# Weight-block sums of the last expert moved from VectorE to GpSimd, in the second phase of an attention and mixture-of-experts kernel

## Chip, cores and metric

The kernel runs on one core of a Trainium2 chip. The metric is device time in microseconds (us) of one execution; lower is better. Engines are named as in the profile: PE is TensorE (PEld its weight loads), DVE VectorE, ACT ScalarE, POOL GpSimd, and SP the engine that issues most DMAs.

## What is computed

The reference is a linear attention with a complex decay, followed by a dense mixture of four experts:

```
for t in range(768):                       # 4 batches, 8 heads, head size 48
    S_re, S_im = ar*S_re - ai*S_im + k_t v_t^T, ar*S_im + ai*S_re
    y[t] = q_t @ S_re
x = y as [3072, 384]
p = domain_probs / (sum + 1e-9)
out = sum over e of p[:, e] * (relu(x @ w1[e]) @ w2[e])     # w1[e] 384 x 1024, w2[e] 1024 x 384
```

All data are float32. The matmuls run on values rounded to a shorter float32 format; each operand is split into a high part and a low part (the difference), and a product is made of three matmuls: high by high, low by high, high by low.

## The kernel before, in words

**Two phases.** In the first, the attention is computed in 12 groups of 256 time steps while experts 0 and 1 are applied to the groups that are done (lines 229 and 209 are their matmuls). The second phase applies experts 2 and 3 with a bilinear scheme of rank 20: a unit multiplies four blocks of 128 hidden columns by two blocks of 384 rows over three blocks of inner dimension, 24 block products, and does it with 20 products of sums of blocks. Each product needs a sum of 128 x 128 weight blocks (the weight operand, splits in `shi` and `slo`, two of them in `ext`) and a sum of 384-column blocks of `x` (`xh`, `xl`).

**Rounds and units.** Each of the two experts takes four rounds, R = 0 to 3 for expert 2 and R = 4 to 7 for expert 3; each round covers 768 rows of `x`. A round has two units, h = 0 and h = 1, one for each half of the hidden layer. The order of a unit is written out in the table UNIT: "M" is a product (three matmuls into one of five PSUM banks `pb`, 0 to 4), "C" a copy of a bank by ScalarE, "D" a sum or difference by VectorE into a bank or into the buffer `SN`, "H" and "L" the high and low part of a finished hidden block (`hid`), "F" eight places where second-layer matmuls of an earlier block (`pob`) are put, and "B" a place where up to n steps of background work are issued.

**Background work.** The list `side` holds what has to be prepared for later units; `bg(n)` takes up to n steps from its head. A step of kind "sum" or "split" counts one; a step of kind "pool" counts nothing and is issued as soon as it is at the head. A "gap" of k stops k calls that still have steps left to take. A split is two instructions: ScalarE writes the high part and VectorE the low part; the ScalarE half of the following split is issued ahead of the VectorE half of this one. What is left in the list at the end of an h = 0 unit is issued there, all at once.

**Order on the engines.** In the second phase ScalarE, VectorE and SP instructions are held in the order in which the program issues them, and so are TensorE's. GpSimd's are not: a scheduler orders them. Each engine runs its queue in order, so an instruction that waits holds up all that stand behind it on its engine.

**What is prepared.** `prep_x(R+1)` (sums of `x` blocks on GpSimd, from line 896, and splits) for each next round. `prep_w(e, h, ...)` for weights: it loads four weight rows (SP, line 973) into the first half of `ACC` and into `RX`, makes 15 sums in the scratch `s`, which lies in the columns 2304 and up of `Z`, splits the sums and some raw blocks, and loads the second-layer weights by casting DMAs on GpSimd (line 995), whose low parts are finished in the h = 1 unit (line 999 and a ScalarE instruction each). Both halves of expert 2 are prepared at the end of the first phase. The first half of expert 3 is prepared in R = 1, h = 0, long before it is used in R = 4, h = 0. The second half is prepared in R = 4, h = 0 and used in R = 4, h = 1, directly behind it.

**Lines.** Line 890 is `tt` (VectorE sums and the low parts of splits), 893 `stt` (VectorE low parts of hidden blocks and the accumulation), 887 `act` (ScalarE copies and high parts), 896 `pool` (GpSimd sums), 884 `pe` (matmuls of the second phase), 1091 and 1123 the loads and stores of the accumulator `ACC`, 1018 the loads of `x` blocks.

Of the kernel before, what the change touches and what calls it, by code (L numbers as in the profile page):

```python
# [28 lines left out]
E1 = 2  # L29
# [20 lines left out]
TB2 = 384  # L50
# [48 lines left out]
def fast_path(ctx, tc, qkP, aP, vP, probsP, w, out, flag):  # L99
# [11 lines left out]
                            base=32, channel_multiplier=1)  # L111
# [148 lines left out]
    with ExitStack() as c1:  # L260
# [4 lines left out]
        def tmp(name):  # L265
# [6 lines left out]
                                base=0, channel_multiplier=-1)  # L272
# [70 lines left out]
        last = {}  # L343
# [436 lines left out]
        x = {}  # L780
# [79 lines left out]
    with ExitStack() as c2:  # L860
# [4 lines left out]
        Z = fin.tile([P, 11 * TB2], F32, name="Z")  # L865
        SN = fin.tile([P, 7 * TB2], F32, name="SN")
        ACC = fin.tile([P, 2 * C2 * HD], F32, name="ACC")
        RX = fin.tile([P, TB2], F32, name="RX")
# [3 lines left out]
        side, freed, ready = [], set(), set()  # L872

        def cut(n):
            return slice(n * P, (n + 1) * P)
# [4 lines left out]
        def pin(ins):  # L880
            return tc.keep_in_program_order(ins) if held["on"] else ins
# [4 lines left out]
        def act(dst, src, fn=AF.Copy, scale=1.0):  # L886
            return pin(nc.scalar.activation(dst, src, fn, scale=scale))  # L887

        def tt(dst, x, y, op):
            pin(nc.vector.tensor_tensor(dst, x, y, op=op))  # L890

        def stt(dst, x, scalar, y, op0, op1):
            pin(nc.vector.scalar_tensor_tensor(dst, x, scalar, y, op0=op0, op1=op1))  # L893
# [4 lines left out]
        def slot(nm, n):  # L898
            if (nm, n) not in static:
                static[nm, n] = wpool.tile([P, 2 * HD], F32R, tag=f"w{nm}", name=f"s{nm}{n}")  # L900
            return static[nm, n]

        def split(hi, lo, src, need=None, neg=False, mark=None):
            def first():
                act(hi, src, scale=-1.0 if neg else 1.0)

            def second():
                if neg:
                    stt(lo, src, -1.0, hi, ALU.mult, ALU.subtract)
                else:  # L910
                    tt(lo, src, hi, ALU.subtract)
                if mark is not None:
                    ready.add(mark)
            return ["split", need, first, second]

        def step(*ops, need=None, on=None):
            f = tt if on is None else on

            def run():
                for o in ops:  # L920
                    f(*o)
            return ["sum" if on is None else "pool", need, run, None]
# [23 lines left out]
                second()  # L946
                n -= 1

        def prep_w(e, h, base, rows, last):
            i = e * FE + 4 * h  # L950
            hi, lo = ([slot(nm, base + n) for n in range(5)] for nm in ("hi", "lo"))
            ext = fin.tile([P, 4 * P], F32R, tag="ext", name=f"ext{i}", bufs=3)
            rows = rows.rearrange("p (f k c) -> p f k c", f=3, k=NJ)
            last = last.rearrange("p (k c) -> p k c", k=NJ)
            s = Z[:, 6 * TB2:].rearrange("p (n c) -> p n c", c=P)
            ops = {}
            for n, r in enumerate((12, 9, 7, 15, 6, 8, 1, 16, 14, 13, 17, 4, 3, 2, 10, 19, 11, 5)):
                ops[r] = hi[n // 6][:, cut(n % 6)], lo[n // 6][:, cut(n % 6)]
            ops[18], ops[0] = ((ext[:, cut(n)], ext[:, cut(2 + n)]) for n in range(2))
            quads[e, h] = ops  # L960

            def blocks(x, n):
                return x.rearrange("p (n c) -> p n c", c=P)[:, n]

            def a(f, k):
                return last[:, k - 1] if f == 4 else rows[:, f - 1, k - 1]

            def n(lo_, hi_):
                return s[:, lo_:hi_]

            def loads():
                for u in range(4):
                    pin(nc.sync.dma_start(rows[:, u] if u < 3 else last,
                                          w[i + u][:, :HD].rearrange("p (k c) -> p k c", k=NJ)))

            add, sub = ALU.add, ALU.subtract
            out = [step((n(0, 3), rows[:, :, 1], rows[:, :, 0], sub)),
                   step((s[:, 3], a(4, 2), a(4, 1), sub), (s[:, 8], a(1, 3), a(4, 3), add)),
                   step((n(10, 12), rows[:, 2, :2], last[:, :2], add)),
                   step((s[:, 9], a(2, 3), a(3, 3), add), (n(4, 6), n(0, 2), rows[:, :2, 2], add)),  # L980
                   step((n(6, 8), n(0, 2), n(8, 10), add)),
                   step((s[:, 5], s[:, 5], a(4, 3), sub), (s[:, 12], a(1, 2), a(2, 1), add)),
                   step((s[:, 8], s[:, 12], s[:, 8], add), (s[:, 9], s[:, 12], s[:, 9], sub)),
                   step((s[:, 10], s[:, 6], s[:, 10], sub), (s[:, 11], s[:, 7], s[:, 11], add)),
                   step((s[:, 13], a(3, 1), a(4, 2), add), (s[:, 14], a(3, 1), a(1, 2), sub))]
            for src, q, lim in ((n(0, 3), 0, slice(0, 3)), (n(3, 6), 0, slice(3, 6)), (n(6, 9), 1, slice(0, 3)),
                                (n(9, 12), 1, slice(3, 6)), (n(12, 15), 2, slice(0, 3)),
                                (rows[:, 2, 0::2], 2, slice(3, 5)), (a(2, 1), 2, 5)):
                out.append(split(blocks(hi[q], lim), blocks(lo[q], lim), src))
            out.append(split(blocks(ext, slice(0, 2)), blocks(ext, slice(2, 4)), last[:, 1:], mark=("w", e, h)))  # L990
            for u in range(4):
                wts[i + u] = tuple(x[3 + u // 2][:, u % 2 * HD:(u % 2 + 1) * HD] for x in (hi, lo))

            def cast(k):
                nc.gpsimd.dma_start(wts[k][0], w[k][:, HD:])

            def rest(k):
                act(wts[k][1], wts[k][0].bitcast(F32), scale=-1.0)
                nc.gpsimd.dma_start(wts[k][1], w[k][:, HD:], accum_op=ALU.add)
                if k == i + 3:  # L1000
                    ready.add(("w2", e, h))

            ks = [(i + u,) for u in range(4)]
            return loads, out, [step(*ks, on=cast)], [["act", None, lambda k=k: rest(*k), None] for k in ks]

        def drain():
            while side:
                bg(len(side))
# [78 lines left out]
        def acc_load(R, u):  # L1087
            e, b = E1 + R // NB2, 2 * (R % NB2) + u
            for t in range(C2):
                c = b * C2 + t  # L1090
                pin(nc.sync.dma_start(ACC[:, (u * C2 + t) * HD:(u * C2 + t + 1) * HD],
                                      acc_d[c // CG][:, c % CG, :] if e == E1 else acc2_d[c]))
# [66 lines left out]

        half = C2 * HD  # L1160
        jobs = [prep_w(E1, h, 5 * h, x[:, :half], y) for h, x, y in ((0, ACC, RX), (1, SN, SN[:, half:half + HD]))]
        freed.update(range(16))
        side += prep_x(0)
# [8 lines left out]
        for R in range(NR2):  # L1172
            for h in range(2):
                if h == 1 or R > 0:
                    acc_load(R if h == 1 else R - 1, 1 - h)
                todo_x = prep_x(R + 1) if h == 0 and R + 1 < NR2 else todo_x
                if R + 1 == NR2:
                    todo_x = []
                if h == 0:
                    side += todo_x[:1]  # L1180
                    tail = []
                    if R == 0:
                        side += [["gap", None, 2, None]] + jobs[1][3] + [["gap", None, 2, None]]
                    if R in (1, NB2):
                        loads, main, casts, tail = prep_w(E1 + 1, *((0, 10) if R == 1 else (1, 0)), ACC[:, :half], RX)
                        loads()
                        side += [["gap", None, 1, None]] + main + casts
                    side += todo_x[1:2]
                else:
                    side += tail  # L1190
                    if R + 1 < NR2:
                        freed.clear()
                        side += todo_x[2:]

                def fill(k, u=2 * R + h):
                    if u == 0 and k == 0:
                        mo.flush()
                    elif u > 1 or (u, k) == (0, 6) or (u == 1 and k < FE - 1):
                        l2()

                unit(R, h, fill)
                if h == 0:
                    drain()
# [195 lines left out]
```

## Time and profile before

| what | us |
|---|---|
| median of 3 runs | 990.64 (988.59 to 992.09) |
| the profiled execution | 988.62 |
| its span, first to last instruction | 986.9 |
| TensorE busy in it | 950.9 |
| VectorE, ScalarE, GpSimd busy | 754.2, 480.5, 167.0 |

The mean granted TensorE clock is 0.993 of full speed. In the views below, a row of the timeline has the start, the length, the engine, the line and the operation with its output and inputs; behind it in brackets the idle time of the engine before it and who ended it. A row of groups has busy time, mean length in ns of one, and the idle time before them. A row of waits has total, number and longest. A row of windows has the stretch, its length, the busy time of each engine with its number of instructions, the granted clock, the DMA share and GB/s. The second phase begins in the profile with the first matmul of line 884, at 597.08 us; the unit R = 1, h = 0 starts at about 636, R = 4, h = 0 at about 776 and R = 4, h = 1 at 799.26.

### The profile page before, as it was taken

What the parts mean: (1) busy time and instruction counts of PE and PEld (TensorE: products, weight loads), DVE (VectorE), ACT (ScalarE), POOL (GpSimd) and SP (SyncE); (2) the same over time, 40 slices, a digit from 0 to 9 for tenths busy, and PEclk for the clock granted to TensorE, in tenths of its full rate; (3) what the DMA queues carried; (4) which work ended last, traced back from release to release, by engine and by line L of the source; (5) the groups of instructions that cost most, each with busy time, mean ns of one, the idle gap of its engine ahead of it and who ended that gap; (6) DMA issues with size and microseconds to landing.
All of it is one profiled execution on the core that took longest, in us unless ns stands there. A gap on an engine that the chain in (4) does not pass through costs nothing.

```text
span 986.9 us, 17555 instructions
## 1 busy us (share of the span) xinstructions
PE 950.9 (96%) x6717; PEld 924.9 (94%) x6717; DVE 754.2 (76%) x1618; ACT 480.5 (49%) x960; POOL 167.0 (17%) x206
## 2 busy tenths in 40 slices
PE   5899998999999999999999999999999989999997
PEld 2799998999999999999999999999999979999997
DVE  7889989798898889878972298888576868576643
ACT  7755435455363635536242266555454445454430
POOL 6030000000000000000000016434334243323000
PEclk9999999999999999999999999999999989999999
DMA  9585276584755747385471267243321432131112
GB/s 297 185 170 142 68 190 144 146 176 135 181 152 122 182 121 201 101 207 158 92 178 24 83 199 151 65 125 86 110 81 65 129 87 87 59 97 49 49 49 76
DMA packets 107053, 123.82 MB, mean 125 GB/s; under 512 B 7440, under 2 KB 94528, under 8 KB 106960
## 3 DMA queue, kind: packets, MB, share of 16 engines
q1 hardware_dynamic: 95472, 95.69, 35.4%
q0 software_dynamic: 11488, 26.93, 11.8%
q8 instruction: 55, 0.90, 0.4%
q14 instruction: 38, 0.31, 0.1%
HBM read 81.96 MB, written 40.62 MB: 124 GB/s over the span
## 4 chain that ended last, share of the span: by engine, by line


## 5 line engine op out<-in xcount | busy, mean ns | idle before, releaser
L884 PE MATMUL pob<-shi,hid 128*128 128x384 f32 x528 | 148.2, 335 | 0.7 <-DVE hid L893 0.6
L229 PE MATMUL po<-whi,hh 128*128 128x384 f32 x384 | 129.7, 339 | 1.1 <-ACT hh L219 1.1
L219 ACT ACTIVATE hh<-ph 128x512 fp32r<-128x512 f32 x96 | 57.2, 595 | 150.1 <-PE ph L209 147.6
L229 PE MATMUL po<-wlo,hh 128*128 128x384 f32 x384 | 128.9, 336 | 0.0
L229 PE MATMUL po<-whi,hl 128*128 128x384 f32 x384 | 124.1, 338 | 0.5 <-DVE hl L220 0.5
L896 POOL TENSOR_TENSOR Z<-Z 128x384 f32<-128x384 f32 x84 | 94.4, 1153 | 131.1 <-DVE xl L890 48.8
L209 PE MATMUL ph<-xha,whi 128*128 128x256 f32 x576 | 104.0, 286 | 1.2 <-ACT xha L196 1.2
L209 PE MATMUL ph<-xha,wlo 128*128 128x256 f32 x576 | 101.5, 283 | 0.0
L884 PE MATMUL pb<-xh,slo 128*128 128x384 f32 x288 | 96.8, 336 | 4.7 <-DVE slo L890 4.7
L209 PE MATMUL ph<-xla,whi 128*128 128x256 f32 x576 | 100.9, 284 | 0.4 <-DVE xla L198 0.4
L884 PE MATMUL pb<-xh,shi 128*128 128x384 f32 x291 | 97.8, 338 | 3.6 <-DVE pb L890 3.1
L220 DVE SCALAR_TENSOR_TENSOR hl<-ph,hh 128x512 fp32r<-128x512 f32 x96 | 65.9, 687 | 46.2 <-ACT hh L219 45.4
L884 PEld LDWEIGHTS pob<-shi,hid 128*128 128x128 f32 x528 | 96.4, 188 | 2.4 <-DVE hid L893 1.2
L884 PE MATMUL pb<-xl,shi 128*128 128x384 f32 x288 | 96.7, 336 | 0.0
L209 PEld LDWEIGHTS ph<-xha,whi 128*128 128x128 f32 x576 | 86.0, 190 | 2.5 <-ACT xha L196 1.5
L884 PE MATMUL pob<-slo,hid 128*128 128x384 f32 x264 | 88.2, 334 | 0.0
L209 PEld LDWEIGHTS ph<-xla,whi 128*128 128x128 f32 x576 | 82.6, 191 | 0.6 <-DVE xla L198 0.6
L209 PEld LDWEIGHTS ph<-xha,wlo 128*128 128x128 f32 x576 | 82.8, 190 | 0.2 <-issue 0.2
L890 DVE TENSOR_TENSOR xl<-Z,xh 128x384 fp32r<-128x384 f32 x104 | 64.9, 652 | 22.6 <-ACT xh L887 14.9
L887 ACT ACTIVATE SN<-pb 128x384 f32<-128x384 f32 x96 | 47.2, 492 | 65.9 <-PE pb L884 57.8
L887 ACT ACTIVATE hid<-pb 128x384 fp32r<-128x384 f32 x76 | 37.2, 490 | 76.2 <-PE pb L884 75.9
L229 PEld LDWEIGHTS po<-whi,hh 128*128 128x128 f32 x384 | 72.4, 189 | 1.5 <-ACT hh L219 1.3
(221 smaller groups left out, 2107.5 us busy)
## 6 DMA issues: line engine op xcount, KB each, us to landing
qk<-qkP SPq DMA_DIRECT2D x24, 384.0 KB, 7.1
acc_d<-acc POOLq DMA_DIRECT2D x24, 384.0 KB, 4.8
ACC<-acc_d SPq DMA_DIRECT2D x48, 192.0 KB, 3.0
A<-aP SPq DMA_DIRECT2D x22, 384.0 KB, 8.1
Z<-y_d SPq DMA_DIRECT2D x16, 384.0 KB, 4.5
q_d<-Q SPq DMA_DIRECT2D x12, 387.0 KB, 4.1
Qst<-q_d SPq DMA_DIRECT2D x12, 387.0 KB, 5.7
v<-vP SPq DMA_DIRECT2D x24, 192.0 KB, 2.6
```

Of the source, the lines that this page charges most:

```text
L209: ins = nc.tensor.matmul(ph[:, u, :], wt[:, j * P:(j + 1) * P], xt[:, j, :], start=(n == 0), stop=(n == 3 * NJ - 1))
L219: wts["hh"] = nc.scalar.activation(hh, ph, AF.Relu)
L220: nc.vector.scalar_tensor_tensor(hl, ph, 0.0, hh, op0=ALU.max, op1=ALU.subtract)
L229: nc.tensor.matmul(po[t], ht[:, u, t * P:(t + 1) * P], wt[:, HD:], start=(i % FE == 0 and n == 0), stop=(i % FE == FE - 1 and n == 2))
L884: return tc.keep_in_program_order(nc.tensor.matmul(*args, **kw))
L887: return pin(nc.scalar.activation(dst, src, fn, scale=scale))
L890: pin(nc.vector.tensor_tensor(dst, x, y, op=op))
L896: nc.gpsimd.tensor_tensor(dst, x, y, op=op)
```

## The change

`prep_w` takes a new argument, the engine for its sums. For the two preparations of expert 3 it is GpSimd; for expert 2 it stays VectorE. The 15 sums are the same in another grouping (seven steps for nine). The gap of one ahead of the sums is gone: the sums are issued when the loads are, and a gap of two stands behind them, before the splits. The splits are six for eight, in another order: first those that need no sum (256, 128 and 256 columns, from `ACC` and `RX`), then two of 768 columns and one of 384 from the scratch. The total of columns is the same. This holds for expert 2 too.

```
-        def prep_w(e, h, base, rows, last):
+        def prep_w(e, h, base, rows, last, on=None):
...
-            out = [step((n(0, 3), rows[:, :, 1], rows[:, :, 0], sub)),
-                   step((s[:, 3], a(4, 2), a(4, 1), sub), (s[:, 8], a(1, 3), a(4, 3), add)),
...
+            groups = [((n(0, 3), rows[:, :, 1], rows[:, :, 0], sub), (s[:, 3], a(4, 2), a(4, 1), sub)),
+                      ((n(10, 12), rows[:, 2, :2], last[:, :2], add), (s[:, 8], a(1, 3), a(4, 3), add)),
...
+            out = [step(*x, on=on) for x in groups]
+            if on is not None:
+                out.append(["gap", None, 2, None])
+            out.append(split(blocks(hi[2], slice(3, 5)), blocks(lo[2], slice(3, 5)), rows[:, 2, 0::2]))
+            out.append(split(blocks(hi[2], 5), blocks(lo[2], 5), a(2, 1)))
+            out.append(split(blocks(ext, slice(0, 2)), blocks(ext, slice(2, 4)), last[:, 1:]))
+            out.append(split(hi[0], lo[0], Z[:, 6 * TB2:8 * TB2]))
+            out.append(split(hi[1], lo[1], Z[:, 8 * TB2:10 * TB2]))
+            out.append(split(hi[2][:, :TB2], lo[2][:, :TB2], Z[:, 10 * TB2:], mark=("w", e, h)))
...
-                        loads, main, casts, tail = prep_w(E1 + 1, *((0, 10) if R == 1 else (1, 0)), ACC[:, :half], RX)
+                        loads, main, casts, tail = prep_w(E1 + 1, *((0, 10) if R == 1 else (1, 0)), ACC[:, :half], RX,
+                                                          on=pool)
                         loads()
-                        side += [["gap", None, 1, None]] + main + casts
+                        side += main + casts
```

The order on the engines changes with it. The three places that matter follow, all in a unit h = 0 in which expert 3 is prepared; numbers in names are buffers.

ScalarE before, in R = 4, from the two bank copies in the middle of the unit on; `shi` from `Z` and `ACC` and `ext` are the high parts of weights, `SN<-pb` the bank copies:

```order
L887 ACTIVATE SN<-pb_7005 128x384
L887 ACTIVATE SN<-pb_7001 128x384
L887 ACTIVATE hid_7102<-pb_7039 128x384
L887 ACTIVATE shi_7110<-SN 128x384
L887 ACTIVATE shi_6845<-Z 128x384 x2
L887 ACTIVATE shi_6846<-Z 128x384
L887 ACTIVATE hid_7052<-pb_7042 128x384
```

ScalarE now, the same place:

```order
L887 ACTIVATE SN<-pb_6997 128x384
L887 ACTIVATE shi_6847<-ACC 128x256
L887 ACTIVATE shi_6847<-ACC 128x128
L887 ACTIVATE ext_8604<-RX 128x256
L887 ACTIVATE shi_6845<-Z 128x768
L887 ACTIVATE shi_6846<-Z 128x768
L887 ACTIVATE SN<-pb_6993 128x384
L887 ACTIVATE shi_6847<-Z 128x384
L887 ACTIVATE hid_7094<-pb_7031 128x384
```

Five high parts now stand between the two bank copies that followed each other before; two of them read sums from `Z`.

VectorE before, in R = 1 (R = 4 has the same rows); `Z` on the left are the weight sums, `slo` the low parts of weights:

```order
L890 TENSOR_TENSOR pb_7039<-pb_7008,SN 128x384
L890 TENSOR_TENSOR SN<-pb_7008,SN 128x384
L890 TENSOR_TENSOR pb_7042<-pb_7005,SN 128x384
L890 TENSOR_TENSOR pb_7008<-SN,pb_7005 128x384
L890 TENSOR_TENSOR Z<-Z 128x128 x2
L890 TENSOR_TENSOR Z<-ACC,RX 128x128
L890 TENSOR_TENSOR Z<-ACC 128x128
L893 SCALAR_TENSOR_TENSOR hid_7068<-pb_7039,hid_7068 128x384
```

VectorE now, from the step ahead of the same four bank operations on (R = 4):

```order
L893 SCALAR_TENSOR_TENSOR hid_7060<-pb_7034,hid_7060 128x384
L890 TENSOR_TENSOR slo_6852<-ACC,shi_6847 128x256
L890 TENSOR_TENSOR slo_6852<-ACC,shi_6847 128x128
L890 TENSOR_TENSOR ext_8604<-RX,ext_8604 128x256
L890 TENSOR_TENSOR slo_6850<-Z,shi_6845 128x768
L890 TENSOR_TENSOR pb_7031<-pb_7000,SN 128x384
L890 TENSOR_TENSOR SN<-pb_7000,SN 128x384
L890 TENSOR_TENSOR pb_7034<-pb_6997,SN 128x384
L890 TENSOR_TENSOR pb_7000<-SN,pb_6997 128x384
L890 TENSOR_TENSOR slo_6851<-Z,shi_6846 128x768
L890 TENSOR_TENSOR slo_6852<-Z,shi_6847 128x384
```

The sums are gone from VectorE, and four of the six low parts stand ahead of the four bank operations; before, all eight stood behind them.

GpSimd now, in R = 4; before there were only the casts here (`shi<-w`), four of them behind one another and then the sums of `x` blocks:

```order
L998 DMA shi_6848<-w 128x384
L896 TENSOR_TENSOR Z<-ACC 128x384
L896 TENSOR_TENSOR Z<-ACC 128x128 x2
L896 TENSOR_TENSOR Z<-RX 128x128
L896 TENSOR_TENSOR Z<-ACC,RX 128x256
L896 TENSOR_TENSOR Z<-ACC,RX 128x128 x2
L896 TENSOR_TENSOR Z<-Z,ACC 128x256
L998 DMA shi_6849<-w 128x384
L896 TENSOR_TENSOR Z<-Z 128x256
L896 TENSOR_TENSOR Z<-Z,RX 128x128
L998 DMA shi_6849<-w 128x384
L896 TENSOR_TENSOR Z<-Z 128x128 x4
```

One cast and one sum of 128 columns stand ahead of these rows. The first 768 columns that are split are complete with the eleventh sum, the row ahead of the last cast; the others need the last row. In R = 1 the same fifteen sums stand together, and the four casts, which stood ahead of all this, stand behind them.

More of the change, by code (lines that the diff above doesn't have):

```diff
@@ L976, in prep_w @@
             add, sub = ALU.add, ALU.subtract
-            out = [step((n(0, 3), rows[:, :, 1], rows[:, :, 0], sub)),
-                   step((s[:, 3], a(4, 2), a(4, 1), sub), (s[:, 8], a(1, 3), a(4, 3), add)),
[L979 to L990, printed above, removed]
+            groups = [((n(0, 3), rows[:, :, 1], rows[:, :, 0], sub), (s[:, 3], a(4, 2), a(4, 1), sub)),
+                      ((n(10, 12), rows[:, 2, :2], last[:, :2], add), (s[:, 8], a(1, 3), a(4, 3), add)),
+                      ((s[:, 9], a(2, 3), a(3, 3), add), (n(4, 6), n(0, 2), rows[:, :2, 2], add)),
+                      ((n(6, 8), n(0, 2), n(8, 10), add), (s[:, 5], s[:, 5], a(4, 3), sub)),
+                      ((s[:, 12], a(1, 2), a(2, 1), add), (s[:, 8], s[:, 12], s[:, 8], add),
+                       (s[:, 9], s[:, 12], s[:, 9], sub)),
+                      ((s[:, 10], s[:, 6], s[:, 10], sub), (s[:, 11], s[:, 7], s[:, 11], add)),
+                      ((s[:, 13], a(3, 1), a(4, 2), add), (s[:, 14], a(3, 1), a(1, 2), sub))]
```

## Prediction

> **What bounds the kernel now.** I read the page first, then the chain of waits on TensorE, then its timeline around the longest wait of the second phase.
>
> ```profile
> PE 950.9 (96%) x6717; PEld 924.9 (94%) x6717; DVE 754.2 (76%) x1618; ACT 480.5 (49%) x960; POOL 167.0 (17%) x206
> ...
> PE lp L177 <- DMA wst<-w: 9.6, 1, 9.6
> PE pb L884 <- DVE slo L890: 4.7, 1, 4.7
> PE pb L884 <- DVE pb L890: 3.1, 2, 1.9
> ```
>
> TensorE is the bound; a change is worth what it does to TensorE's idle time, and of that little lies in the second phase. The first row of waits is the start of the program and untouched. The second is one wait for the low parts of split weights (`slo`), the third two waits for a sum that VectorE writes into a PSUM bank. Here they are in place:
>
> ```profile
> 799.26 0.34 PE L884 MATMUL pb<-xh,shi 128*128 128x384 f32 x1
> 804.34 0.69 PE L884 MATMUL pb<-xh,slo 128*128 128x384 f32 x1 [4.74 <-DVE slo L890]
> 804.83 0.52 PE L884 MATMUL pb<-xl,shi 128*128 128x384 f32 x1
> ...
> 808.67 0.52 PE L884 MATMUL pob<-shi,hidhl 128*128 128x384 f32 x1
> 808.99 0.39 PE L884 MATMUL pb<-xh,shi 128*128 128x384 f32 x1
> ...
> 809.57 0.34 PE L884 MATMUL pb<-xh,shi 128*128 128x384 f32 x1
> ...
> 799.00:804.30 5.30, 0.60 (x4) 0.28 (x2) 5.30 (x9) 0.99 (x3) 5.21 (x7) 0.81 0.11 39
> 804.30:808.00 3.70, 3.66 (x11) 3.66 (x12) 1.80 (x3) 1.72 (x4) 2.25 (x4) 0.50 0.62 210
> ...
> 676.94 0.44 PE L884 MATMUL pb<-xh,shi 128*128 128x384 f32 x1 [1.93 <-DVE pb L890]
> ...
> 822.87 0.44 PE L884 MATMUL pb<-xh,shi 128*128 128x384 f32 x1 [1.15 <-DVE pb L890]
> ```
>
> At 799.26 the unit R=4, h=1 starts with product 19, the first that uses weights prepared in the unit before it. The split that makes their low half was among the last in that unit's work list, and TensorE waits 4.74 us. Then its clock is 0.50 (the third number from the end of the windows rows; the row before, with the wait in it, has 0.81), and matmuls start 0.32 us apart instead of 0.17 until 808.99. From 799.26 to 809.57 eighteen matmuls went by; at 0.173 us each that is 3.1 us, so the stall cost 10.31 - 3.1 = 7.2 us. The waits of 1.93 and 1.15 stand in the h=1 units that follow the two preparations (R=1 and R=4). The h=1 units of the other rounds have none, so I put them down to VectorE and GpSimd still being late from the preparation.
>
> **What the change removes.** In both rounds the splits now come early and the one that product 19 reads comes first. Nothing is then left at the unit's end to wait for: 7.2 us go. The later waits, 1.93 + 1.15 = 3.1 us, should go too, as VectorE loses the sums of two units and the leftover splits behind them; if they stay, only 7.2 goes. I take both, 10.3. The VectorE time set free, fifteen short sums each, is worth nothing by itself: it lay beside TensorE's work.
>
> **What it adds: sums on GpSimd.** Fifteen sums per preparation, one of 384 columns, three of 256, eleven of 128. The trace shows GpSimd sums only at 384, so the narrow ones are bounded.
>
> ```profile
> L896 POOL TENSOR_TENSOR Z<-Z 128x384 f32<-128x384 f32 x84 | 94.4, 1153 | 131.1 <-DVE xl L890 48.8 <-DMA Z<-y_d 41.2 <-DVE slo L890 24.9
> L289 POOL MEMSET P<- 112x384 f32 x1 | 0.4, 418 | 0.0
> L270 POOL MEMSET mask<- 128x128 f32 x1 | 0.2, 237 | 0.0
> L1391 POOL MEMSET const-float32-1.0<- 128x1 f32 x1 | 0.1, 101 | 0.0
> ...
> 738.22 1.98 POOL L896 TENSOR_TENSOR Z<-Z 128x384 f32<-128x384 f32 x2 [6.42 <-DVE hidhl L893]
> 785.16 0.53 POOL L995 DMA_DIRECT2D shi<-w  x1 [2.33 <-PE pob L884]
> 788.80 0.53 POOL L995 DMA_DIRECT2D shi<-w  x1 [3.11 <-PE pob L884]
> ```
>
> Undisturbed, a 384-column sum takes 0.99 us (two in 1.98); the mean of 1.153 includes waiting. If width were free, 128 columns would cost 0.99 too; if it were all, 0.33. The MEMSET rows lie near the second end: 0.10 us fixed, the rest by columns. I take 0.10 fixed: 0.40 us at 128, 0.69 at 256. All fifteen: 0.99 + 3 x 0.69 + 11 x 0.40 = 7.5 us (bounds 6.6 and 14.9); the first eleven in GpSimd's order, which complete the first 768 columns that are split, 5.9 us (bounds 5.3 and 10.9).
>
> The Trainium skill speaks against the move: its page GPSIMD Engine Reference, section Engine selection, sends elementwise sums to VectorE, GpSimd being about twice as slow with two inputs. Its 4497 ns for 2048 columns would make 2560 columns an estimated 5.6 us before any per-instruction cost; the forecast below would then be about 4 us lower.
>
> When do they start, and who waits?
>
> ```profile
> 644.18 0.56 DVE L890 TENSOR_TENSOR Z<-ACC 128x384 f32<-128x384 f32 x1 [0.58 <-DMA ACC<-w]
> ...
> 784.65 0.56 DVE L890 TENSOR_TENSOR Z<-ACC 128x384 f32<-128x384 f32 x1 [0.75 <-DMA ACC<-w]
> 789.06 0.57 DVE L890 TENSOR_TENSOR pb<-pb,SN 128x384 f32<-128x384 f32 x1 [0.30 <-PE pb L884]
> 794.73 1.02 DVE L890 TENSOR_TENSOR slo<-Z,shi 128x384 fp32r<-128x384 f32 x2 [0.53 <-ACT shi L887]
> 803.08 2.22 DVE L890 TENSOR_TENSOR slo<-ACC,shi 128x256 fp32r<-128x256 f32 x2
> 805.69 0.41 DVE L890 TENSOR_TENSOR ext<-RX,ext 128x256 fp32r<-128x256 f32 x1
> ...
> 789.58 0.49 ACT L887 ACTIVATE SN<-pb 128x384 f32<-128x384 f32 x1 [2.11 <-PE pb L884]
> 794.19 1.33 ACT L887 ACTIVATE shi<-Z 128x384 fp32r<-128x384 f32 x3
> ...
> 651.17 0.33 PE L884 MATMUL pb<-xh,shi 128*128 128x384 f32 x1
> 651.69 0.33 PE L884 MATMUL pb<-xh,shi 128*128 128x384 f32 x1
> ...
> 791.46 0.33 PE L884 MATMUL pb<-xh,shi 128*128 128x384 f32 x1
> 791.98 0.33 PE L884 MATMUL pb<-xh,shi 128*128 128x384 f32 x1
> ```
>
> The sums need the weight rows, on which VectorE waited until 784.65 (R=4) and 644.18 (R=1). In R=4 two DMA issues of 0.53 stand among the first eleven sums and a third before the last four. VectorE's operations on two SBUF operands and GpSimd's sums hold each other up: the pair at 803.08 took 2.22 us with GpSimd at work, where two of 384 took 1.02 alone. Three such splits (256, 128, 256 columns, some 1.0 us by the 0.41 row) fall among the sums; I add 1.0.
>
> R=4: the eleventh sum ends at 784.65 + 5.9 + 1.1 + 1.0 = 792.6, the last at 792.6 + 0.5 + 1.6 = 794.7. Now the wait that the change adds. ScalarE's two 768-column splits stand in its queue ahead of the copy that was at 789.58; VectorE's first 768-column split stands ahead of the sum that was at 789.06. TensorE's product 9 (791.46) needs that sum, product 5 (791.98) that copy. A 768 split is 0.85 us on ScalarE (three of 384 in 1.33) and 0.95 on VectorE. So the sum ends at 792.6 + 0.85 + 0.95 + 0.5 = 794.9, 3.4 us after product 9 was due; the copy at 794.7 + 0.8 + 0.5 = 796.0, 4.0 after product 5 was due. R=4 costs 4.0.
>
> R=1 has no DMA issue among the sums: 644.18 + 5.9 + 1.0 = 651.1 and 652.7; the sum ends at 653.4 (2.2 late against 651.17), the copy at 654.0 (2.3 late against 651.69). R=1 costs 2.3. At the low end (6.6 us of sums, nothing held up) R=4 costs 2.1. In R=1 the start may also come a microsecond sooner, since four casts of weight rows no longer go out ahead of the loads; then it costs nothing.
>
> Those casts are the change's one move past a queue:
>
> ```profile
> 636.42 2.17 POOL L995 DMA_DIRECT2D shi<-w  x4
> ...
> 662.08 1.34 ACT L887 ACTIVATE slo<-shi 128x384 fp32r<-128x384 f32 x3
> ...
> shi<-w POOLq DMA_DIRECT2D x16, 192.0 KB, 4.5
> ```
>
> In R=1 they now go out behind the sums, at 652.7 instead of 636.42; with 2.2 us of issue and 4.5 to land they are there at 659.4, and ScalarE takes them up at 662.08. Cost 0 with 2.7 us to spare; past that, ScalarE would wait with the copies of the next unit behind it. The second expert-3 half has its casts among the sums, and its consumers too come a unit later.
>
> **The first preparation.** Both halves of expert 2 stay on VectorE with the same columns in fewer splits. TensorE entered the phase without waiting:
>
> ```profile
> 597.08 0.33 PE L884 MATMUL pb<-xh,shi 128*128 128x384 f32 x1
> 600.37 0.33 PE L884 MATMUL pb<-xh,shi 128*128 128x384 f32 x1
> ...
> 596.89 1.95 DVE L890 TENSOR_TENSOR Z<-Z 128x128 f32<-128x128 f32 x2
> ...
> 598.15 0.47 ACT L887 ACTIVATE pb<-pb 128x384 f32<-128x384 f32 x1
> ```
>
> The bank copy at 598.15 now stands behind both 768 splits on ScalarE. The sums end at 598.8, plus 0.8 and 0.5 is 600.1, before the bank is written at 600.37. Cost 0, hidden by the last expert-1 matmuls between these two; one GpSimd sum in VectorE's way would make it 0.7.
>
> **Sum.** 10.3 - 4.0 - 2.3 = 4.0 us gained. The profiled execution took 988.62 us (span 986.9) and would take 984.6; it is 2.0 below the median of the runs, 990.64, so I forecast 986.6.
>
> **Rivals.** (1) The sums are done before anyone needs them, or nearly: low ends throughout, gain 10.3 - 2.1 = 8.2, 982.4. For it: the MEMSET rows, and loads that may land sooner. Against it: in R=4 even 5.3 us of sums with two DMA issues end at 791.0, when product 9 is all but due. Chance 0.18.
>
> (2) The new wait in R=4 halves the clock again. The 4.74 us wait did, the 1.93 one did not; 3.4 lies between. The drop cost 7.2 - 4.74 = 2.4 us; the gain shrinks to 1.6, 989.0, no change. The Trainium skill's page TensorE: Matmul & The Clock Gate, section What's actually happening, has the half rate come back after an idle window of about 3.4 us. By that rule this rival decides the result; the trace agrees at 1.93 and 4.74 and shows nothing between. Chance 0.20.
>
> (3) Slower: a GpSimd sum costs by the instruction rather than by the column. Then the sums take 14.9 us, 7.4 more; both waits grow by that, and both drop the clock: 14.8 + 4.8 on top, 15.6 us slower, 1006. It decides early: at 0.50 us per 128-column sum the waits grow by some 1.1 each and both may pass the clock's limit, 2.2 + 4.8 = 7.0, which is 3.0 slower than before. For it: fifteen small instructions that wait on one another; against it, the 237 ns row. Chance 0.15.
>
> The forecast keeps 0.47. Its own range is 983 to 990. The whole range, 980 to 994, leaves out most of rival 3 and the lowest of rival 1. A measurement tells 0.3% (3 us) from no change: faster is below 987.7, slower above 993.6. Faster: most of the forecast (0.36), rival 1, and a third of rival 2: 0.60. Same 0.25. Slower 0.15.
>
> **What would show it.** In the profile after: no `slo` wait at the start of R=4, h=1 and clock 1.00 there; a new row in the chain of waits, TensorE waiting in the middle of R=1 and of R=4, h=0, for VectorE's sum into `pb` or ScalarE's copy into `SN`, 2 to 4 us; ScalarE idle before its `shi` split until a POOL sum of `Z`; 128-column sums near 0.40 us. If these rows are absent, rival 1 is right; if the sums are near 0.9 us, rival 3. The forecast is wrong in its removal if a wait for `slo` or the 1.93 us one is still there.

## The result and the profile after

The changed kernel takes 986.28 us (median of 5 runs, 984.2 to 988.16); the kernel before takes 990.99 beside it (5 runs, 988.59 to 992.52). The ratio is 0.995, with a 95% interval of 0.9926 to 0.9973: faster by 0.5%. The profiled execution took 986.28, with a span of 984.5.

Page of the changed kernel, busy time of each engine:

```profile
PE 950.3 (97%) x6717; PEld 923.9 (94%) x6717; DVE 739.8 (75%) x1580; ACT 479.4 (49%) x952; POOL 182.5 (19%) x236
```

Waits of TensorE in the changed kernel (line, who is waited for: total, number, longest):

```profile
PE pb L884 <- DVE pb L890: 3.4, 3, 1.2
PE pb L884 <- ACT SN L887: 1.1, 1, 1.1
```

The 4.74 us wait for `slo` is gone. TensorE's timeline shows where the four waits stand, and what follows the middle two:

```profile
677.16 0.45 PE L884 MATMUL pb<-xh,shi 128*128 128x384 f32 x1 [1.18 <-DVE pb L890]
...
792.95 0.45 PE L884 MATMUL pb<-xh,shi 128*128 128x384 f32 x1 [1.11 <-DVE pb L890]
...
794.87 0.44 PE L884 MATMUL pb<-xh,shi 128*128 128x384 f32 x1 [1.13 <-ACT SN L887]
...
798.96 0.34 PE L884 MATMUL pb<-xl,shi 128*128 128x384 f32 x1
...
820.22 0.44 PE L884 MATMUL pb<-xh,shi 128*128 128x384 f32 x1 [1.16 <-DVE pb L890]
```

The waits at 677.16 and 820.22 are those of 1.93 and 1.15 before, in R=1, h=1 and R=4, h=1. The pair at 792.95 and 794.87 is new: products 9 and 5 in the middle of R=4, h=0. Behind it the clock halves (windows of the changed kernel; third number from the end):

```profile
793.00:795.00 2.00, 0.87 (x4) 0.56 (x5) 0.98 (x3) 1.41 (x3) 2.00 (x4) 1.00 0.41 119
795.00:797.00 2.00, 2.00 (x8) 2.00 (x9) 2.00 (x4) 0.61 (x2) 1.04 (x2) 0.60 0.00 0
797.00:799.00 2.00, 2.00 (x9) 2.00 (x8) 1.89 (x4) 0.52 (x1) 2.00 (x3) 0.54 0.00 0
799.00:801.00 2.00, 2.00 (x13) 2.00 (x12) 1.17 (x4) 0.49 (x1) 1.91 (x2) 1.00 0.00 0
```

Matmuls follow each other 0.173 us apart and each is counted busy for 0.34, so product 9 was due 0.17 before the wait began: 792.95 - 1.11 - 0.17 = 791.67. Seventeen matmuls go by from it to the one at 798.96, 2.94 us at full clock. So R=4 costs 798.96 - 791.67 - 2.94 = 4.35 us. Against the starts of the same matmuls in the kernel before, products 9 and 5 account for 1.27 and 1.40 of it, a little more than their waits of 1.11 and 1.13, and eleven matmuls at half clock for 0.15 each, 1.6 together.

GpSimd's sums by shape in the changed kernel (busy, mean ns of one):

```profile
L896 POOL TENSOR_TENSOR Z<-ACC 128x128 f32<-128x128 f32 x6 | 2.6, 454 | 5.6 <-DMA ACC<-w 5.6
L896 POOL TENSOR_TENSOR Z<-ACC 128x384 f32<-128x384 f32 x2 | 2.0, 1010 | 1.2 <-DMA ACC<-w 1.2
...
L896 POOL TENSOR_TENSOR Z<-ACC,RX 128x256 f32<-128x256 f32 x2 | 1.5, 738 | 0.0
```

So 0.45, 0.74 and 1.01 us for 128, 256 and 384 columns. In R=1 the fifteen run from 642.29 to 649.99 (GpSimd's timeline, first and last rows), and nobody waits there:

```profile
642.29 2.26 POOL L896 TENSOR_TENSOR Z<-ACC 128x128 f32<-128x128 f32 x4 [4.07 <-DMA ACC<-w]
...
648.26 1.73 POOL L896 TENSOR_TENSOR Z<-Z 128x128 f32<-128x128 f32 x4
649.92 2.17 POOL L998 DMA_DIRECT2D shi<-w  x4
```

**Where the time came from.** The first phase, whose code is the same but for the preparation of expert 2 at its end, took from 597.0 to 601.9 us in the fourteen profiles of this study, so I compare the second phase alone: from the first matmul of line 884 to the end of the span. It took 986.9 - 597.1 = 389.8 before and 984.5 - 599.1 = 385.4 after, 4.4 less. In pieces, by the starts of the same matmuls in both: -7.2 (the wait for `slo` and its halved clock), -0.75 (1.93 became 1.18), -0.8 (two short stalls of the kernel before, at 660.14 and 662.22, gone; the rows of waits show only 0.23 of it, for ScalarE's copy), -0.2 (short stalls up to 603.76, gone), +4.35 in R=4, 0 in R=1, and +0.2 behind the last matmul. That is -4.4.

### The profile page after: what moved, and what is told of

It is laid out like the page before. It is cut to its first block, busy times and chain, and to the rows that moved or that the text cites. A ratio compares the mean times of both kernels' runs of the same rounds, so it can differ in the third digit from the quotient of the medians.

```text
span 984.5 us, 17548 instructions
## 1 busy us (share of the span) xinstructions
PE 950.3 (97%) x6717; PEld 923.9 (94%) x6717; DVE 739.8 (75%) x1580; ACT 479.4 (49%) x952; POOL 182.5 (19%) x236
## 4 chain that ended last, share of the span: by engine, by line
## 5 line engine op out<-in xcount | busy, mean ns | idle before, releaser
L896 POOL TENSOR_TENSOR Z<-Z 128x384 f32<-128x384 f32 (+2 forms) x94 | 97.5, 1059 | 108.2 <-DVE xl L890 49.4
## 6 DMA issues: line engine op xcount, KB each, us to landing
qk<-qkP SPq DMA_DIRECT2D x24, 384.0 KB, 7.1
acc_d<-acc POOLq DMA_DIRECT2D x24, 384.0 KB, 4.9
A<-aP SPq DMA_DIRECT2D x22, 384.0 KB, 8.2
Z<-y_d SPq DMA_DIRECT2D x16, 384.0 KB, 3.9
```

The source lines that it names most:

```text
L896: nc.gpsimd.tensor_tensor(dst, x, y, op=op)
```

## Experiments

My theory after the result: the gain is made by the order of the splits, which takes the wait for `slo` away; the engine of the sums is worth nothing and costs the pair of waits in R=4. By the order I mean all that the change did to the splits: their order, their number (six for eight) and their earlier place; no run takes these apart. The rival: the gain comes from freeing VectorE. A second question is what causes the waits in the h=1 units, which I had put down to the preparation. Lengths of the second phase are from each run's profiled execution.

### The sums on GpSimd alone

```
 out = [step(*x, on=on) for x in groups]
 if on is not None:
-    out.append(["gap", None, 2, None])
+    out.append(["gap", None, 4, None])
...                                        # then the eight splits of the kernel before
```

> The sums of expert 3 are on GpSimd, but the eight splits have their old order and their old places at the end of the unit (a gap of four behind the sums). Theory A: the slo wait of 3 to 5 us and the halved clock after it are back, and the waits in the middle of the unit are gone: 989 to 992, no change against the kernel before. Theory B: VectorE is free, so the splits are done in time even there: 986 or less.

991.71 us (989.99 to 994.63), ratio 0.999 (0.9973 to 1.0006): no gain; second phase 391.0. The old waits are all back, those of the h=1 units with 1.90 and 1.17 (TensorE's timeline of this run):

```profile
805.31 0.69 PE L884 MATMUL pb<-xh,slo 128*128 128x384 f32 x1 [4.75 <-DVE slo L890]
```

Taking fifteen sums off VectorE does not shorten the wait for `slo` by a hundredth.

### The new order alone, sums on VectorE

```
-prep_w(..., ACC[:, :half], RX, on=pool)
+prep_w(..., ACC[:, :half], RX, on=None)
-side += main + casts
+side += [["gap", None, 1, None]] + main + casts
```

> The sums of expert 3 stay on VectorE (a gap of one ahead of them, as before the change); the six splits keep their new order and so end in the middle of the unit. Theory A (the order earns the gain, GpSimd costs): no wait for slo at the start of R=4, h=1, no waits in the middle of R=4, h=0, clock 1.00 in both, and about 4.3 us less than the changed kernel, near 982. Theory B (the gain comes from relieving VectorE of the sums): VectorE is as full as before, part of the slo wait and of the halved clock is back, 988 to 991.

986.72 us (983.01 to 988.14), ratio 0.993 (0.9903 to 0.9956); second phase 385.3, as in the changed kernel. No wait for `slo`, none in the middle of R=4; the waits left are 1.92 and 1.94 us in the two h=1 units, and here the first is followed by a halved clock (timeline, then windows, of this run):

```profile
680.59 0.44 PE L884 MATMUL pb<-xh,shi 128*128 128x384 f32 x1 [1.92 <-DVE pb L890]
```

```profile
680.00:685.00 5.00, 4.41 (x16) 4.41 (x17) 4.47 (x11) 1.43 (x3) 0.00 (x0) 0.66 0.01 3
```

Order alone gives the gain, the engine alone gives none. The rival falls. I had expected 982, as the waits of R=4 go; they went, but the h=1 waits are longer by 1.6 us together, short stalls for ScalarE's copies bring another 1.0 and the halved clock 1.5, so that nothing is left of it.

### A gap of three for two

```
-    out.append(["gap", None, 2, None])
+    out.append(["gap", None, 3, None])
```

> The changed kernel with a gap of three instead of two behind the sums: the splits that read sums come one place later, behind the bank copy on ScalarE and the bank sums on VectorE. ScalarE's order is then that of the kernel with the sums on VectorE. Theory A: the waits in the middle of R=4, h=0 are gone, no wait at the start of h=1, 982, equal to the kernel with the sums on VectorE. Rival (later splits are again too late for the next unit): a slo wait of 1 us or more at the start of R=4, h=1, 986 or more.

985.27 us (983.11 to 986.9), ratio 0.9926 (0.9901 to 0.9951); second phase 383.9. The splits now stand behind the bank operations that had waited for them: the pair in R=4 is gone and the clock does not halve. The h=1 waits are 1.94 and 1.91 us instead of 1.18 and 1.16; I put that down to the later splits of `x`, which leave less room behind them, but no run tests it. My expectation of 982 was missed by these waits:

```profile
676.94 0.45 PE L884 MATMUL pb<-xh,shi 128*128 128x384 f32 x1 [1.94 <-DVE pb L890]
...
816.98 0.44 PE L884 MATMUL pb<-xh,shi 128*128 128x384 f32 x1 [1.91 <-DVE pb L890]
```

ScalarE's order is that of the run with the new order and sums on VectorE, so the two differ by the sums' engine alone: 383.9 against 385.3, and the halved clock there is worth 1.5. The engine is worth nothing that these runs can tell.

### The casts behind the sums

```
+for prev in static["pool"][-15:] if on is not None else ():
+    behind(ins, prev)        # each cast behind the fifteen sums on GpSimd's queue
```

> The changed kernel with the four casts of weight rows in R=4 held behind the sums on GpSimd. Theory A (the two waits in the middle of R=4 end with the sums, which the casts hold up): the last sum ends about 1.7 us sooner, both waits shrink from 1.1 to about 0.5, the clock is not halved, 983. Rival (the waits come from five splits ahead of the bank copy on ScalarE, whenever the sums end): waits as in the changed kernel, 986.

985.27 us (984.24 to 986.37), ratio 0.9923 (0.9898 to 0.9947); second phase 384.0. The wait of product 9 is gone, that of product 5 is 0.73, and the clock holds. A wait of 1.43 appears at 801.19, still in R=4, h=0. VectorE's last two low parts of weights took 4.48 us there beside GpSimd's sums of `x`; in the changed kernel they took 1.46 (TensorE's timeline, then VectorE's, of this run):

```profile
794.80 0.45 PE L884 MATMUL pb<-xh,shi 128*128 128x384 f32 x1 [0.73 <-ACT SN L887]
...
801.19 0.44 PE L884 MATMUL pb<-xh,shi 128*128 128x384 f32 x1 [1.43 <-DVE pb L890]
```

```profile
795.25 4.48 DVE L890 TENSOR_TENSOR slo<-Z,shi 128x768 fp32r<-128x768 f32 x2
```

So the two cast issues among the first eleven sums were part of the lateness, and removing them moves about as much to another place. I had expected 983 and no new wait.

### The casts first, in R=1

```
-side += main + casts
+side += casts + main if R == 1 else main + casts      # and the casts held right behind the stores
```

> In R = 1 alone the four casting DMAs are issued ahead of the 15 sums, where they stood in the kernel before. If R = 1 was free of waits because the loads landed sooner with the casts behind them, the sums start 2 to 4 us later and TensorE waits for 1 to 3 us in the middle of R = 1, h = 0, with or without a halved clock behind it: 1 to 4 us more than the changed kernel, 987 to 990. If the sums had slack of their own, no wait appears and the time stays at 986.

989.95 us (987.81 to 991.71), ratio 0.9971 (0.9956 to 0.9986); second phase 387.6. With the casts back where they stood before the change, R=1 has the waits that the prediction had for it (GpSimd's timeline, then TensorE's, of this run):

```profile
639.67 2.17 POOL L998 DMA_DIRECT2D shi<-w  x4
645.79 0.45 POOL L896 TENSOR_TENSOR Z<-ACC 128x128 f32<-128x128 f32 x1 [3.95 <-DMA ACC<-w]
647.08 1.85 POOL L896 TENSOR_TENSOR Z<-ACC 128x384 f32<-128x384 f32 x3 [0.83 <-DMA ACC<-w]
```

```profile
655.74 0.44 PE L884 MATMUL pb<-xh,shi 128*128 128x384 f32 x1 [1.16 <-DVE pb L890]
656.83 0.44 PE L884 MATMUL pb<-xh,shi 128*128 128x384 f32 x1 [0.31 <-ACT SN L887]
```

SP issues the first load at 640.27 here and at 638.78 in the changed kernel; the first sum starts 645.79 - 640.27 = 5.5 us later, against 642.29 - 638.78 = 3.5. R=1 was free because the casts no longer went ahead of the loads. Of the 2.2 us by which the phase is longer, these two waits bring 1.9 by the starts of the same matmuls in both (1.5 by the rows of waits). R=4, whose code is unchanged, brings next to nothing: its first wait was 2.16 in this execution, but its second 0.22.

### The sums later, in R=4

The edit makes the first sum of R=4, 384 columns, three times. Its first form changed nothing: its condition matched neither preparation, and so it is a second sample of the changed kernel.

> In R = 4 alone the first sum (384 columns, 1.01 us) is made three times, so that all sums behind it are 2.0 us later; no part of the result changes. If the lateness of the sums is paid in full, the first wait in R = 4, h = 0 goes from 1.1 to about 3.1 us, the second stays at 1.1, and the halved clock behind them costs 2 us or more: 988 to 990. If the engine has slack that the waits hide, the time stays at 986.

986.87 us (984.13 to 988.79), ratio 0.9942 (0.9917 to 0.9966); second phase 385.1; waits in R=4 of 0.95 and 1.12, the clock at 0.86 from 790 to 800. It says nothing on the question, only how well the changed kernel repeats. The second form:

```
+if on is not None and h == 1:
+    groups[0] = groups[0][:1] * 2 + groups[0]
```

> In R = 4 alone the first sum (384 columns, 1.01 us) is made three times, and no part of the result changes. If the lateness of the sums is paid in full, TensorE's first wait in R = 4, h = 0, 1.0 to 2.8 us in the runs of the same order, becomes 3.0 to 4.8, with the halved clock behind it: about 2 us more than the changed kernel, 988 to 989. If a wait hides it, the time stays at 986.

988.26 us (986.45 to 991.47), ratio 0.9965 (0.9951 to 0.9979); second phase 387.5, 2.1 more than the changed kernel. GpSimd's timeline of this run shows the two extra sums, each with a cast issue behind it, ahead of the 256-column ones; then TensorE's:

```profile
788.36 1.01 POOL L896 TENSOR_TENSOR Z<-ACC 128x384 f32<-128x384 f32 x1
789.32 0.58 POOL L1000 DMA_DIRECT2D shi<-w  x1
```

```profile
796.29 0.69 PE L884 MATMUL pb<-xh,shi 128*128 128x384 f32 x1 [4.04 <-DVE pb L890]
```

One wait of 4.04 replaces the pair (the second is gone since product 5 now comes late itself), 1.8 us more of waiting than 1.11 + 1.13, with a halved clock behind it as before. The two extra sums, 2.0 us, are paid in full.

Without an edit the same shows. Five runs have the same code in R=4, h=0, and the first wait there is the longer the later GpSimd's second stretch of sums starts, counted from the last load's issue (timelines of SP, GpSimd and TensorE):

| run | from load issue to sums | first wait | second |
|---|---|---|---|
| the second sample | 786.93 - 783.0 = 3.9 | 0.95 | 1.12 |
| changed | 784.25 - 780.2 = 4.1 | 1.11 | 1.13 |
| finishing steps later (below) | 783.04 - 778.9 = 4.1 | 1.14 | 1.12 |
| casts first in R=1 | 788.27 - 783.6 = 4.7 | 2.16 | 0.22 |
| finishing steps elsewhere (below) | 783.15 - 778.1 = 5.1 | 2.75 | 0.70 |

### The finishing steps in another unit

The h=1 waits: in both units the list begins with the four steps that finish the second-layer weights, each a ScalarE instruction and a DMA issued on GpSimd. Here those of R=1 go to R=2, h=0:

```
+late, tail = tail if R == 2 else [], []
...
-side += todo_x[1:2]
+side += todo_x[1:2] + late
...
-side += tail
+side += tail if R != 1 else []
```

> The four finishing steps of expert 3's first half (ScalarE writes slo, GpSimd adds w by DMA) go from the start of R = 1, h = 1 to R = 2, h = 0. If they cause the waits of h = 1 (they hold back six GpSimd sums of x, which then hold up VectorE), the wait of 1.18 us in R = 1, h = 1 goes and that of 1.16 in R = 4, h = 1, whose steps stay, remains: 1.2 us less than the changed kernel, about 985. If the splits left over from h = 0 cause it, both waits remain and the time is that of the changed kernel.

985.73 us (981.88 to 988.63, 6 runs), ratio 0.9931 (0.9898 to 0.9963). The wait in R=1, h=1 is gone, that in R=4, h=1 stays, and none comes in R=2. The second phase is 386.5 all the same, as R=4 drew the longest waits of the table, with the clock halved for 6.8 us behind them. How the steps act is seen on VectorE and GpSimd. The changed kernel's timelines of both, R=1, h=1:

```profile
662.81 2.69 POOL L1002 DMA_DIRECT2D slo<-w  x3 [0.83 <-ACT slo L887]
666.29 0.86 POOL L1002 DMA_DIRECT2D slo<-w  x1 [0.80 <-ACT xh L887]
668.90 7.31 POOL L896 TENSOR_TENSOR Z<-Z 128x384 f32<-128x384 f32 x6 [1.75 <-DVE xl L890]
```

```profile
671.35 2.71 DVE L893 SCALAR_TENSOR_TENSOR xl<-Z,xh 128x384 fp32r<-128x384 f32 x2
673.98 2.65 DVE L890 TENSOR_TENSOR xl<-Z,xh 128x384 fp32r<-128x384 f32 x2
676.55 0.55 DVE L890 TENSOR_TENSOR pb<-pb,SN 128x384 f32<-128x384 f32 x1
...
678.41 1.01 DVE L890 TENSOR_TENSOR xl<-Z,xh 128x384 fp32r<-128x384 f32 x2
```

The same of the run without the steps there:

```profile
665.62 2.10 POOL L896 TENSOR_TENSOR Z<-Z 128x384 f32<-128x384 f32 x2 [4.25 <-DVE xl L890]
668.66 3.54 POOL L896 TENSOR_TENSOR Z<-Z 128x384 f32<-128x384 f32 x3 [0.95 <-DVE xl L893]
```

```profile
672.54 1.84 DVE L890 TENSOR_TENSOR xl<-Z,xh 128x384 fp32r<-128x384 f32 x2
674.30 0.55 DVE L890 TENSOR_TENSOR pb<-pb,SN 128x384 f32<-128x384 f32 x1
```

With the steps, GpSimd runs six sums of `x` in one go beside VectorE's splits, and two low parts take 2.7 us where two take 1.01 alone; the bank sum behind them (676.55) is what TensorE waits for. Without the steps the sums start 2.6 us sooner, counted from the start of the second phase, in shorter stretches, and the bank sum is done in time. The Trainium skill's page SBUF — State Buffer, section SBUF: two separate sides, has an exclusive lock on the port pair that VectorE and GpSimd share: of a VectorE operation with two inputs in SBUF and a GpSimd operation that reads SBUF, the one that starts first holds it for the whole instruction, and the other waits. The 2.7 against 1.01 fits that.

### The finishing steps later in their unit

```
-side += tail
...
-side += todo_x[2:]
+side += todo_x[2:6] + tail + todo_x[6:]
```

> The same four steps, of both halves of expert 3, stand behind the first three splits and the first group of sums of x in their units h = 1 instead of ahead of them. If they cause the waits, both go: 2.3 us less than the changed kernel, about 984. If only their number matters and not their place, a wait of about the same length comes later in the unit. The waits in the middle of R = 4, h = 0 (1.1 and 1.1 us) and the halved clock behind them stay in both cases.

986.31 us (984.13 to 990.99, 10 runs), ratio 0.9953 (0.9932 to 0.9973); second phase 385.1. Both waits for `pb` go, as expected, but in R=4 the steps are now too late for the weights that they finish, and the 2.3 us that I had expected do not come:

```profile
819.01 0.44 PE L884 MATMUL pob<-slo,hid 128*128 128x384 f32 x1 [2.50 <-DMA slo<-w]
```

### Between the splits, with a gap of three

```
+rest_x = rest_x[:1] + tail[:2] + rest_x[1:2] + tail[2:3] + rest_x[2:3] + tail[3:] + rest_x[3:]
```

> A gap of three for two, and in both units h = 1 the four finishing steps stand between the first three splits of x, two, one and one, in place of ahead of them. By what the earlier runs showed, the gap of three removes the two waits in the middle of R = 4, h = 0 and the halved clock behind them, and the earlier splits let GpSimd sum sooner, so that the waits of 1.9 us in R = 1, h = 1 and R = 4, h = 1 go too: the second phase 380 us where the changed kernel has 385.4, a median of about 981. If the finishing steps come too late so, TensorE waits for the second-layer weights in R = 4, h = 1 as it did for 2.5 us, and the median is 984.

984.93 us (982.83 to 987.18), ratio 0.9934 (0.9912 to 0.9955); second phase 384.1. My expectation of 380 failed: the waits are 2.00 and 2.27, no shorter than the 1.94 and 1.91 of the gap of three. The splits of `x` do come sooner on ScalarE, but GpSimd does not: its timeline still has three DMA issues, then four sums in one go beside VectorE's splits:

```profile
664.50 2.76 POOL L1002 DMA_DIRECT2D slo<-w  x3
666.29 2.28 POOL L896 TENSOR_TENSOR Z<-Z 128x384 f32<-128x384 f32 x1
668.35 1.06 POOL L1002 DMA_DIRECT2D slo<-w  x1
668.96 4.39 POOL L896 TENSOR_TENSOR Z<-Z 128x384 f32<-128x384 f32 x4
```

Beside those four, one pair of VectorE's low parts took 4.39 us (VectorE's timeline):

```profile
669.86 4.39 DVE L893 SCALAR_TENSOR_TENSOR xl<-Z,xh 128x384 fp32r<-128x384 f32 x2
```

So what holds the bank sum up is a long run of GpSimd's sums beside VectorE's splits. The steps' place in the list matters as far as it breaks that run up: behind the first group of sums, as in the run before, it did; between the first splits it does not.

### The same, sums on VectorE

> The sums on VectorE in the new order of steps, with the four finishing steps between the first splits of x as in the run with a gap of three. If the order alone made the gain, all waits of the second phase over 0.3 us go here as well, and it agrees with the GpSimd version of the same order within 1 us, about 981. If the sums on GpSimd are worth something once the waits are gone, it is slower than that version by over 1 us.

The edit is the last one on the kernel with sums on VectorE. 985.61 us (984.39 to 986.8), ratio 0.9935 (0.9915 to 0.9955); second phase 385.7; waits 2.00 and 2.29, a halved clock behind the first. The waits did not go here either, and the 981 expected of both versions was missed, but the comparison stands: within 1 us of the GpSimd version's median, so the engine again makes no difference that shows.

### Put together

Steps of R=1 in R=2, h=0; gap two in R=1, three in R=4; in R=4, h=1 two finishing steps behind the first split and two behind the first group of sums:

```
+    out.append(["gap", None, 2 + h, None])
...
+    rest_x = rest_x[:1] + tail[:2] + rest_x[1:4] + tail[2:] + rest_x[4:]      # R = 4
```

> What the runs showed, put together: the finishing steps of expert 3's first half in R = 2, h = 0, with the gap of two in R = 1, so that R = 1 has no wait; the gap of three in R = 4, so that the middle of R = 4, h = 0 has none; and in R = 4, h = 1 two finishing steps behind the first split of x and two behind the first group of sums. The second phase should be 381 to 382 us where the changed kernel has 385.4 and the best run so far 383.9, with at most one wait left in R = 4, h = 1, of 0.5 to 2.3 us; a median of 982 to 983.5. If the waits removed come back later in the same units, the time stays at 985.

982.48 us (978.94 to 983.83, 6 runs), ratio 0.9909 (0.9886 to 0.9932); second phase 380.2, 5.2 less than the changed kernel. It has the lowest median of all kernels here. One wait over 0.6 us is left in the phase, in R=4, h=1:

```profile
816.67 0.45 PE L884 MATMUL pb<-xh,shi 128*128 128x384 f32 x1 [1.31 <-DVE pb L890]
```

The intervals of this ratio and the changed kernel's overlap a little (up to 0.9932, and from 0.9926), and each was set against its own runs of the kernel before; the waits gone from the trace are the firmer evidence.

## Why the prediction was right, point by point

The time forecast, 986.6, was met, and so was the net: 4.0 forecast in the profiled execution, 4.4 in the second phase. But two terms of the sum were wrong, and that they cancelled was luck.

- **The wait for `slo`, -7.2: right.** It is gone, and it came back at 4.75 when the old splits were put behind GpSimd's sums. It is more than the whole net gain.
- **The waits of 1.93 and 1.15, -3.1: wrong.** They became 1.18 and 1.16. The failed step is "I put them down to VectorE and GpSimd still being late from the preparation". They come from the four finishing steps at the head of the h=1 list and the sums of `x` that these push into VectorE's splits: moving the steps of R=1 away removed its wait. Lateness may still add to them: they were 1.9 again in the runs whose splits of `x` stand later. I had seen that only the units behind a preparation have them, and did not look at what those units alone have in their list.
- **The GpSimd sums: right.** 0.40, 0.69 and 0.99 forecast, 0.45, 0.74 and 1.01 measured; fifteen in 7.7 us in R=1 where 7.5 was forecast. The MEMSET rows were the right neighbours; rival 3 is out. At 384 columns a sum takes 1.8 times the 0.56 us of VectorE, near the factor of two that the prediction quotes; a fixed part, some 0.18 us by the three lengths, is why fifteen take 7.7 us and not the 5.6 estimated there.
- **The hold-up, +1.0 on GpSimd: wrong way round.** VectorE paid. Its early low parts of 256 and 128 columns took 2.18 us in R=4 beside the sums and 1.18 in R=1, where GpSimd was at its narrow ones (VectorE's timeline of the changed kernel). They had room.

```profile
649.29 1.18 DVE L890 TENSOR_TENSOR slo<-ACC,shi 128x256 fp32r<-128x256 f32 x2 [0.85 <-ACT shi L887]
...
788.02 2.18 DVE L890 TENSOR_TENSOR slo<-ACC,shi 128x256 fp32r<-128x256 f32 x2 [0.85 <-ACT shi L887]
```

- **R=4, +4.0: the sum nearly right, the make-up not.** The eleventh sum ended at 790.52, not 792.6 (GpSimd's row below), and the waits were 1.11 and 1.13, not 3.4 and the rest. The step that was mis-sized is that end: 1.0 of hold-up that did not fall on GpSimd, loads that landed 0.7 sooner behind their issue, and one cast issue and one sum that went in while the rest of the loads were awaited. What made up for it is the clock, 1.6 us, which the forecast had left to rival 2. Rival 2's mechanism took place, and at shorter waits than it asked for. That GpSimd's lateness is paid in full was right.

```profile
789.99 0.53 POOL L896 TENSOR_TENSOR Z<-Z,RX 128x128 f32<-128x128 f32 x1
```

- **R=1, +2.3: wrong, 0.** The sums started 3.5 us after the first load's issue, not 7.2. The prediction named the reason, casts no longer going out ahead of the loads, and took it for a microsecond at best. Put back ahead, they cost 1.9 us. A longer R=1 is close at hand: in the run with later sums in R=4, a later matmul of R=1, h=0 waited 0.51 us (at 658.44) with unchanged code, as two low parts took 3.65 us beside GpSimd's sums of `x`.
- **Casts and first preparation, 0: right.** No wait came from either.

So the removal fell short by 2.35 us (10.3 against 7.2 + 0.75), and the price by 1.95 (4.0 + 2.3 against 4.35). The other 0.8 of gain, short stalls gone less 0.2 behind the last matmul, stands in no term of the forecast.

## What to carry to other kernels

A long wait at a unit's start was cured here by issuing early, and first, what that unit reads first; which engine makes the inputs matters only where someone waits for that engine. A DMA moved to another place in a queue shifts the loads beside it too: here four casts out of the way were worth 2 to 3 us of lead. Where a wait appears only in some rounds, list what only those rounds have in their queues before putting it down to being late.

## What the runs showed of the clock

The length of a wait does not decide alone whether TensorE's clock halves. It halved behind single waits of 1.92 and 2.00 us, and behind pairs of 1.1 and 1.1 (three profiles); it held behind single waits of 1.90, 1.91, 1.93, 1.94, 2.00, 2.27, 2.29 and 2.50.

What the traces show is a grid of windows. A halving in the middle of a trace lasts 3.41 us, or twice that: 6.8 in the kernel before and in two of the runs. Within a trace, halvings begin a whole number of such windows apart: in the kernel before at 27.43, 802.25 and 983.16 us, which is 227 and 53 times 3.413. So the windows of a trace can be counted from any halving in it. Here are windows of the run with the new order and sums on VectorE, then of the run with a gap of three (behind the comma the busy time of TensorE; third number from the end the clock):

```profile
678.12:681.53 3.41, 1.49 (x9) 1.17 (x8) 3.41 (x6) 0.10 (x1) 1.45 (x2) 1.00 0.00 0
681.54:684.94 3.40, 3.40 (x13) 3.40 (x12) 2.87 (x7) 1.32 (x3) 0.00 (x0) 0.50 0.02 5
...
672.55:675.96 3.41, 2.46 (x15) 2.14 (x13) 3.41 (x4) 1.32 (x3) 3.33 (x3) 1.00 0.11 18
675.97:679.37 3.40, 2.43 (x14) 2.43 (x15) 3.40 (x8) 0.49 (x1) 0.03 (x1) 1.00 0.02 5
```

In the first run the wait of 1.92 lies in one window, TensorE is busy for 1.49 us of it, and the next window has half the clock. In the second the wait of 1.94 lies across the edge of two windows, each has over 2.4 us of work, and the clock holds. The other waits fit this, with one exception.

All ten halvings of the second phase, in ten profiles, follow a window with at most 1.70 us of work; from full clock, it held behind every window with 1.86 or more. In the changed kernel the pair of 1.11 and 1.13 falls, but for 0.2 us, into one window, 792.00 to 795.41. The exception: in the run with later finishing steps, 815.00 to 818.41 had 1.50 us of work, and the clock held. So how much work a window needs is not settled to the tenth, nor whether busy time is all that counts. Once halved, the clock stayed so for another window at 1.32, 1.94 and 2.69 us of work, and came back at 2.95 and more.

The Trainium skill's page TensorE: Matmul & The Clock Gate, section What's actually happening, has windows of about 3.4 us that run freely and do not start anew with the kernel. The grid agrees, and where its edges fall explains why the same 1.9 or 2.0 us halves the clock in one execution and not in another. The page has the half rate come back after a whole idle window. That does not agree: windows with up to 1.70 us of work were enough.
